# Laying out the first four chunks of a fused RWKV-5 and SwiGLU kernel anew: loading, tables, rounding and the order of the first blocks

## The chip, the cores and the metric

One core of one Trainium2 chip. The metric is device time in microseconds of one execution, lower is better. Times below are medians of several executions; a profile is one execution, and its span is about 1 to 2.5 us shorter than the time of the same execution.

Names: PE is TensorE (PEld its weight loads), DVE VectorE, ACT ScalarE, POOL GpSimd, SP SyncE.

## The reference

```python
# attention, B=4, H=8, S=768, D=48: y_t = r_t (state + u*k_t v_t^T); state = w*state + k_t v_t^T
x = attn_out.transpose(0, 2, 1, 3).reshape(B * S, H * D)          # 3072 x 384
rms = np.sqrt(np.mean(x * x, axis=-1, keepdims=True) + 1e-06)
xn = x / rms * rms_g
g = xn @ w_gate                                                   # 384 x 1536
out = (g / (1 + np.exp(-g)) * (xn @ w_val)) @ w_out               # 1536 x 384
```

The three large weights come as float64. The kernel loads them as 64-bit words and rounds them to float32 itself.

## The kernel before

The sequence is cut into 12 chunks of 64 tokens (times 4 batches). Chunks 0 and 1 are computed alone while the weights still arrive, later chunks in pairs ("pair blocks", 2 and 3 first). In the traces read here, PE, DVE and ACT instructions run in the program's order on each engine, so an instruction that stands early in the program holds up everything behind it on its engine.

The attention of a chunk is called by letters: `1 2 3` the bonus (TOK, TOK times u, reduced to du), `R K` the decayed r and k on DVE, `d` the diagonal (16 small ACT products a half), `a` the scores (tile pa), `m` the mask, `y` the outputs (py), `q r n` squares, root and norm (pm, rms, xa, xb), `h` the K-hat products (KH), `u` the state (pu). A capital means the second half.

```python
def decay_r(s):                                                    # "R"
    dve.tensor_mul(ME, CH[:, 0], ...up...)
    act.copy(MO[64:128], ME[64:128])
def decay_k(s):                                                    # "K"
    dve.tensor_mul(CH[:, 1], CH[:, 1], ...down...)
def diagonal(s, half):                                             # "d": eight products into ME, eight into MO
    ...
    act.mul(t[rows, b, p, :], dmask[rows], du[rows, x : x + 1])

def round_piece():                                                 # 24 pieces: 6 for each quarter of the weights
    dst, raw = staged.popleft()
    ...
    act.activation(ulp, lo, AF.Copy, scale=2.0**-29)
    dve.tensor_scalar(out=bits, in0=hi, scalar1=3, scalar2=0x3FFFFFF8, ...)
    dve.scalar_tensor_tensor(out=bits, in0=hi, scalar=-0x40000000, in1=bits, ...)
    nc.gpsimd.tensor_tensor(out=dst.bitcast(I32), in0=bits, in1=ulp, op=ALU.add)
    stage()                                                        # issues the load of the next piece

def gate_val(s, nn):                                               # needs pieces 0-3 of its quarter
    product(ps_, unit(wa[i], o), xa[s], True)
    product(ps_, unit(wb[i], o), xb[s], False)
    act.activation(h, ps_[:, 0, 0:NT], AF.Silu)
    dve.tensor_mul(h, ps_[:, 1, 0:NT], h)
# add_cell(q, s): h of three gate_val times a quarter of w_out; needs pieces 4 and 5 of its quarter

def check():                                                       # 48 of these, through ONE buffer: weights in range?
    raw = mine.tile([P, CHECK], I64, name=f"again_{n}", tag="again")
    nc.sync.dma_start(out=raw, in_=src[:, k * CHECK : (k + 1) * CHECK])
    act.activation(mag, hi, AF.Abs)
    act.activation(mag, mag, AF.Relu, ..., accum_out=seen[:, n : n + 1])
# at the end: bad = reduction of seen; every engine loads bad and branches (a general kernel for odd inputs)
```

The whole kernel:

## Time and profile before

| | |
|---|---|
| time | 748.5 us (median of 4, 747.7 to 749.4) |
| profiled span | 747.5 us |
| first b product of the pair blocks | 236.9 us |
| last projection product (po) ends | 740.0 us |
| TensorE before that first b, from 14 us on | 157.9 us busy, 65.0 us idle |
| TensorE at half clock before that first b | 75.6 us |

How to read it: the last three quarters of the kernel run TensorE nearly without a hole. The first b product: the first product of the pair blocks that needs sums of both chunks, so a good marker of where the beginning ends. "Idle" and "half clock" are taken from the trace: gaps between matmuls, and the records of the granted clock, which are 1.0 or 0.5.

### The profile page before, as it was taken

The page shows a single profiled execution, that of the slowest core. Times are in us where ns is not written, and L with a number is a line of the kernel's source. Part 1 is how long each engine was busy: PE and PEld are TensorE (multiplying, and loading weights), DVE is VectorE, ACT ScalarE, POOL GpSimd, SP SyncE. Part 2 cuts the span into 40 slices and gives each one's busy share as a digit, 9 for nine tenths or more (in the row PEclk, how much of TensorE's full clock was granted, in tenths as well). Part 3 has the DMA queues.
Part 4 walks back from the last instruction along what each step waited for, and adds up shares of the span by engine and source line. Part 5 has one row for each costly group of instructions (what it writes and reads, how often), then busy time and mean ns, then how long its engine had stood idle before and what let it go on. Part 6 is the DMA issues. An engine that isn't in the chain of part 4 may idle for free.

```text
span 747.5 us, 14896 instructions
## 1 busy us (share of the span) xinstructions
PE 654.6 (88%) x6326; PEld 502.6 (67%) x6326; DVE 400.3 (54%) x569; ACT 341.4 (46%) x945; POOL 45.1 (6%) x40
## 2 busy tenths in 40 slices
PE   2378468796697999999999999999999999999996
PEld 1255256564575778667888668887678886688853
DVE  5836355344537874736675646657257646445410
ACT  1443543534523352545565725746545647244400
POOL 4323112021100000000000000000000000000000
PEclk9768689897899999999999999999999999999999
DMA  8635245053042003242243413153431332022201
GB/s 220 169 108 164 63 107 174 7 132 108 12 116 59 1 1 86 49 101 70 63 130 83 89 55 96 51 148 78 98 73 51 111 87 65 22 59 65 64 21 26
DMA packets 20571, 61.31 MB, mean 82 GB/s; under 512 B 3984, under 2 KB 7056, under 8 KB 19344
## 3 DMA queue, kind: packets, MB, share of 16 engines
q1 hardware_dynamic: 20496, 60.28, 31.0%
q8 instruction: 51, 0.84, 0.5%
q14 instruction: 24, 0.20, 0.1%
HBM read 55.54 MB, written 4.72 MB: 81 GB/s over the span
## 4 chain that ended last, share of the span: by engine, by line
PE 77%; DVE 10%; ACT 5%; issue 4%; DMA 2%; POOL 1%; DVEq 0%; POOLq 0%; ACTq 0%
PE po L89 25%; PE b L89 14%; PE a L89 9%; PE gv L89 9%; PE c L89 8%; PE py L89 5%; PE pa L89 4%; PE pu L89 3%; DVE bits L89 2%; DVE gv L89 1%; ACT MO L89 1%; DMA chan<-in_chan_dram 1%; DVE rms L89 1%; DVE TOK L89 1%; DVE h L89 1%
## 5 line engine op out<-in xcount | busy, mean ns | idle before, releaser
L89 PE MATMUL po<-wo,h 128*128 128x384 f32 x576 | 199.4, 499 | 2.6 <-POOL wo L204 2.6
L89 PEld LDWEIGHTS po<-wo,h 128*128 128x128 f32 x576 | 108.6, 193 | 73.9 <-POOL wo L204 3.9
L89 DVE TENSOR_TENSOR gv<-b,m 128x512 f32<-128x512 f32 x90 | 62.1, 690 | 64.3 <-PE b L89 63.6
L89 PE MATMUL pa<-ME,chan 48*64 48x64 f32 x384 | 31.1, 240 | 32.3 <-issue 18.2
L89 PEld LDWEIGHTS pa<-ME,chan 48*64 48x64 f32 x384 | 27.9, 152 | 41.8 <-issue 39.6
L89 ACT ACTIVATE gv<-gv 128x512 f32<-128x512 f32 (+1 forms) x60 | 31.1, 519 | 48.7 <-DVE gv L89 48.7
L89 PE MATMUL gv<-xa,wa 64*128 64x256 f32 x288 | 47.6, 464 | 4.4 <-DVE xa L89 4.4
L89 DVE TENSOR_TENSOR h<-gv,h 128x256 f32<-128x256 f32 x24 | 10.2, 424 | 74.8 <-ACT h L89 74.7
L89 DVE TENSOR_TENSOR gv<-c,gv 128x512 f32<-128x512 f32 x60 | 41.4, 690 | 15.4 <-PE c L89 14.3
L89 ACT ACTIVATE ME<-dmask,du 64x64 f32<-64x64 f32 x176 | 43.8, 330 | 12.1 <-DVE du L89 11.6
L89 PE MATMUL a<-xa,wa 64*128 64x256 f32 x360 | 45.1, 383 | 4.7 <-DVE h L89 4.7
L89 PE MATMUL b<-t,s 64*128 64x256 f32 x360 | 45.4, 386 | 4.0 <-DVE t L89 3.7
L89 PE MATMUL b<-xa,wa 64*128 64x256 f32 x360 | 45.5, 385 | 0.6 <-DVE gv L89 0.6
L89 PE MATMUL b<-t,wb 64*128 64x256 f32 x360 | 44.5, 379 | 0.8 <-DVE gv L89 0.8
L89 ACT ACTIVATE MO<-dmask,du 64x64 f32<-64x64 f32 x176 | 44.4, 335 | 0.4
L89 PE MATMUL c<-xb,s 64*128 64x256 f32 x360 | 44.3, 378 | 0.0
L89 PEld LDWEIGHTS py<-ME,VS 128*64 128x64 f32 (+1 forms) x576 | 36.4, 136 | 11.3 <-issue 10.7
L89 PE MATMUL c<-t,s 64*128 64x256 f32 x360 | 43.9, 376 | 0.0
L89 PE MATMUL a<-xb,wb 64*128 64x256 f32 x360 | 43.9, 376 | 0.0
L89 PE MATMUL gv<-xb,wb 64*128 64x256 f32 x288 | 40.1, 407 | 3.1 <-POOL wb L204 3.1
L89 PE MATMUL py<-ME,VS 128*64 128x64 f32 (+1 forms) x576 | 39.9, 229 | 2.5 <-DVE MO L89 2.5
L89 PEld LDWEIGHTS gv<-xa,wa 64*128 64x128 f32 x288 | 32.7, 227 | 13.7 <-DVE xa L89 4.8
(101 smaller groups left out, 1049.5 us busy)
## 6 DMA issues: line engine op xcount, KB each, us to landing
TOK<-in_tok_dram SPq DMA_DIRECT2D x12, 768.0 KB, 4.5
chan<-in_chan_dram SPq DMA_DIRECT2D x24, 384.0 KB, 6.4
VS<-in_vpad_dram SPq DMA_DIRECT2D x24, 336.0 KB, 4.8
raw<-in_wka_dram SPq DMA_DIRECT2D x8, 576.0 KB, 4.3
raw<-in_wkb_dram SPq DMA_DIRECT2D x8, 576.0 KB, 3.9
raw<-in_wot_dram SPq DMA_DIRECT2D x8, 576.0 KB, 3.8
again<-in_wka_dram SPq DMA_DIRECT2D x16, 288.0 KB, 2.8
out_dram<-o SPq DMA_DIRECT2D x48, 96.0 KB, 2.2
```

Of the source, the lines that this page charges most:

```text
L89: return lambda *args, **kwargs: self.tc.keep_in_program_order(give(*args, **kwargs))
```

## The change

Its intent: have chunk 1's attention done while TensorE works on the first quarter of the weights, ahead of the second quarter; build tables and K-hat early; keep more float64 pieces in flight; keep TensorE's clock up with products of constants where it would idle. Two sets of checks move as well.

```diff
-    raws = loading.enter_context(tc.tile_pool(name="raws", bufs=3))
+    raws = loading.enter_context(tc.tile_pool(name="raws", bufs=6))
...
-            nc.sync.dma_start(out=wraw[...], in_=w_v[z])           # w, u, g: now from ACT's queue
+            act.dma_start(out=wraw[...], in_=w_v[z])
...
-    def token_tables():                                            # tables and K-hat constants: now at once
...
+    def warm(n):
+        t = ps_gv.tile([P, P], FP32, name=f"warm_{len(warmed)}", tag="c")
+        for _ in range(n):
+            pe.matmul(t, ones, ones, start=True, stop=True)
...
-    mix(0, "RK123aAdmyDMY")
-    rounding(2), mix(0, "qr"), rounding(2), mix(0, "n"), token_tables()
-    gate_val(0, 0), rounding(1), mix(0, "h")
-    gate_val(0, 1), rounding(1), mix(0, "Hu")
-    gate_val(0, 2), mix(0, "U"), rounding(2)
-    add_cell(0, 0), rounding(2)
-    gate_val(0, 3), mix(1, "12")
-    gate_val(0, 4), mix(1, "3Rd")
-    gate_val(0, 5), mix(1, "K"), rounding(1), mix(1, "aDm"), rounding(1)
-    add_cell(1, 0), mix(1, "AMyY"), ...
+    warm(20)
+    mix(0, "123RKaAdmyDM"), rounding(2), mix(0, "Yhq"), warm(4), mix(0, "rHuU")
+    rounding(2), mix(0, "n"), warm(16)
+    gate_val(0, 0), rounding(1), mix(1, "12")
+    gate_val(0, 1), mix(1, "3Rd")
+    gate_val(0, 2), mix(1, "K"), rounding(1), mix(1, "aD")
+    add_cell(0, 0), mix(1, "mAyMYhHqruU"), rounding(2), mix(1, "n"), warm(8)
+    gate_val(1, 0), rounding(1)
+    gate_val(1, 1), rounding(1)
+    gate_val(1, 2), rounding(1)
+    add_cell(0, 1), rounding(1)
+    gate_val(0, 3), mix(2, "1")
+    gate_val(0, 4), mix(2, "2")
+    gate_val(0, 5), mix(2, "3")
+    add_cell(1, 0), mix(2, "Rd")
+    gate_val(1, 3), mix(2, "K")
+    gate_val(1, 4), mix(2, "aDm"), rounding(1)
+    gate_val(1, 5), mix(2, "AM")
+    add_cell(1, 1), mix(2, "y"), rounding(1), mix(2, "Y"), rounding(2)
...                                                                 # chunk 3 in the same way
-                if not first_block and k in (2, 5):
+                if not first_block and k in (2, 5) and m != 2:
                     check()
...
-                project(s, j, False), project(s, j, True)
+                project(s, j, False), project(s, j, True), check(), check()
```

Not in this cut, but in the change: TOK's load goes out ahead of chan's, a Sqrt of a constant loads ACT's table early, and half of chunk 1's diagonal products (those into ME) move from ACT to DVE.

More of the change, by code (lines that the diff above doesn't have):

```diff
@@ L124, in fast @@
     dve.memset(wraw, 1.0)
+    eps = c_tile([P, 1], "eps")
+    dve.memset(eps, EPS)
     w_v = w.rearrange("(a e) d -> e d a", e=2)
@@ L127, in fast @@
         for z in range(2):
-            nc.sync.dma_start(out=wraw[64 * z : 64 * z + D, :], in_=w_v[z])
-    wcol = c_tile([P, HP], "wcol")
-    dve.tensor_scalar(out=wcol, in0=wraw, scalar1=W_LOW, scalar2=W_HIGH, op0=ALU.max, op1=ALU.min)
+            act.dma_start(out=wraw[64 * z : 64 * z + D, :], in_=w_v[z])
     CH = c_tile([P, 2, B, HP, L], "chan")
@@ L148, in load_v @@
         nc.sync.dma_start(out=VS[0:64, 1], in_=vpad[s, 0:64])
+    utab = c_tile([P, HP, D], "utab")
+    gcol = c_tile([P, CC], "gcol")
     for z in range(2):
-        nc.gpsimd.memset(CH[64 * z + 32 : 64 * z + 64], 0.0)
+        (dve, nc.gpsimd)[z].memset(CH[64 * z + 32 : 64 * z + 64], 0.0)
+    load_tok(0)
     load_chan(0)
-    load_tok(0)
-    utab = c_tile([P, HP, D], "utab")
     for z in range(2):
         src = bass.AP(tensor=u.tensor, offset=u.offset + z * D, ap=[[0, 64], [2 * D, HP], [1, D]])
-        nc.sync.dma_start(out=utab[64 - 64 * z : 128 - 64 * z], in_=src)
+        act.dma_start(out=utab[64 - 64 * z : 128 - 64 * z], in_=src)
+    act.dma_start(out=gcol, in_=g_cols)
+    spare = c_tile([P, 1], "spare")
+    act.activation(spare, eps, AF.Sqrt)
     wa = [c_tile([P, CC, NQ * P], f"wa_{i}") for i in range(WQ)]
@@ L212, in fast @@
     load_v(0)
-    stage()
-    stage()
-    stage()
-    gcol = c_tile([P, CC], "gcol")
-    nc.sync.dma_start(out=gcol, in_=g_cols)
+    for _ in range(6):
+        stage()
     ident = c_tile([P, P], "ident")
@@ L223, in fast @@
     nc.gpsimd.memset(ones, 1.0)
-    eps = c_tile([P, 1], "eps")
-    dve.memset(eps, EPS)
+    nc.gpsimd.memset(KH[32:64, 0], 0.0)
+    nc.gpsimd.memset(KH[96:128, 1], 0.0)
+    wcol = c_tile([P, HP], "wcol")
+    dve.tensor_scalar(out=wcol, in0=wraw, scalar1=W_LOW, scalar2=W_HIGH, op0=ALU.max, op1=ALU.min)
     dmask, mask = c_tile([P, L], "dmask"), c_tile([P, L], "mask")
@@ L238, in fast @@
     nc.gpsimd.memset(VS[64:128, 1], 0.0)
-    nc.gpsimd.memset(KH[32:64, 0], 0.0)
-    nc.gpsimd.memset(KH[96:128, 1], 0.0)
     pw = raws.tile([P, HP, L], FP32, name="pw", tag="pw", bufs=1)
@@ L262, in fast @@
     dve.tensor_add(dmask, ident[:, 0:64], ident[:, 64:128])
-    def token_tables():
-        for z in range(2):
-            dve.tensor_mul(gdup[:, :, z, :], pw_rev, free_dims(pows[L // 2], (1, HP), (0, L)))
-        ps = ps_at.tile([P, HP, P], FP32, name="ps_wk", tag="at")
-        for p in range(HP):
-            pe.transpose(ps[:, p, :], gdup[:, p].rearrange("c z t -> c (z t)"), ident)
-        act.copy(wk[64:128], ps[64:128, :, 0:D])
-        act.copy(wk[0:64], ps[0:64, :, 64 : 64 + D])
-        for z in range(2):
-            rows = slice(64 * z, 64 * z + D)
-            for p in range(HP):
-                act.mul(
-                    KH[rows, z, :, p, :], free_dims(ident[rows, 64 * z : 64 * z + D], (0, B), (1, D)),
-                    pows[L][rows, p : p + 1],
-                )
+    for z in range(2):
+        dve.tensor_mul(gdup[:, :, z, :], pw_rev, free_dims(pows[L // 2], (1, HP), (0, L)))
+    ps = ps_at.tile([P, HP, P], FP32, name="ps_wk", tag="at")
+    for p in range(HP):
+        pe.transpose(ps[:, p, :], gdup[:, p].rearrange("c z t -> c (z t)"), ident)
+    act.copy(wk[64:128], ps[64:128, :, 0:D])
+    act.copy(wk[0:64], ps[0:64, :, 64 : 64 + D])
+    for z in range(2):
+        rows = slice(64 * z, 64 * z + D)
+        for p in range(HP):
+            act.mul(
+                KH[rows, z, :, p, :], free_dims(ident[rows, 64 * z : 64 * z + D], (0, B), (1, D)),
+                pows[L][rows, p : p + 1],
+            )
     def w_range():
@@ L319, in diagonal @@
         for t, rows in ((ME, slice(64, 128)), (MO, slice(0, 64))):
-            if s == 0:
+            if s == 0 or (s == 1 and t is ME):
                 dve.tensor_mul(
@@ L517, in rounding @@
             round_piece()
-    mix(0, "RK123aAdmyDMY")
-    rounding(2)
-    mix(0, "qr")
-    rounding(2)
-    mix(0, "n")
-    token_tables()
-    gate_val(0, 0), rounding(1), mix(0, "h")
-    gate_val(0, 1), rounding(1), mix(0, "Hu")
-    gate_val(0, 2), mix(0, "U"), rounding(2)
-    count = w_range()
-    add_cell(0, 0), rounding(2)
-    gate_val(0, 3), mix(1, "12")
-    gate_val(0, 4), mix(1, "3Rd")
-    gate_val(0, 5), mix(1, "K"), rounding(1), mix(1, "aDm"), rounding(1)
-    add_cell(1, 0), mix(1, "AMyY"), rounding(1), mix(1, "qr"), rounding(1), mix(1, "n")
@@ L534, in fast @@
-    gate_val(1, 0), rounding(1), mix(1, "h")
-    gate_val(1, 1), mix(1, "Hu"), rounding(1)
-    gate_val(1, 2), mix(1, "U"), rounding(1)
-    add_cell(0, 1), mix(2, "12")
-    gate_val(1, 3), mix(2, "3Rd")
-    gate_val(1, 4), mix(2, "K")
-    gate_val(1, 5), mix(2, "aDm")
-    add_cell(1, 1), mix(2, "A"), rounding(1), mix(2, "M")
-    gate_val(0, 6), mix(2, "y"), rounding(1)
-    gate_val(0, 7), mix(2, "Y")
-    gate_val(0, 8), mix(2, "q"), rounding(1), mix(2, "r")
-    add_cell(2, 0), mix(2, "n")
@@ L546, in fast @@
-    gate_val(1, 6), mix(2, "hHu"), rounding(1)
-    gate_val(1, 7), mix(2, "U"), rounding(1)
-    gate_val(1, 8), mix(3, "12")
-    add_cell(2, 1), mix(3, "3Rd"), rounding(1)
-    gate_val(0, 9), mix(3, "K"), rounding(1)
-    gate_val(0, 10), mix(3, "aDm")
-    gate_val(0, 11), rounding(1), mix(3, "AM")
-    rounded(len(pieces))
+    def warm(n):
+        t = ps_gv.tile([P, P], FP32, name=f"warm_{len(warmed)}", tag="c")
+        warmed.append(t)
+        for _ in range(n):
+            pe.matmul(t, ones, ones, start=True, stop=True)
@@ new lines, in fast @@
+    warmed = []
+    warm(20)
[5 more added lines that the diff above has]
+    add_cell(0, 0), mix(1, "mAyMYhHqruU"), rounding(2), mix(1, "n"), warm(8)
+    count = w_range()
+    gate_val(1, 0), rounding(1)
+    gate_val(1, 1), rounding(1)
+    gate_val(1, 2), rounding(1)
+    add_cell(0, 1), rounding(1)
@@ new lines, in fast @@
+    gate_val(0, 3), mix(2, "1")
[6 more added lines that the diff above has]
+    add_cell(1, 1), mix(2, "y"), rounding(1), mix(2, "Y"), rounding(2)
+    gate_val(0, 6), mix(2, "qr")
+    gate_val(0, 7), mix(2, "n")
+    gate_val(0, 8), rounding(2), mix(2, "h")
+    add_cell(2, 0), mix(2, "Hu"), rounding(1)
+    gate_val(1, 6), mix(2, "U"), mix(3, "1")
@@ L554, in fast @@
+    gate_val(1, 7), mix(3, "2"), rounding(1)
+    gate_val(1, 8), mix(3, "3Rd")
+    add_cell(2, 1), mix(3, "K"), rounding(1), mix(3, "aD"), rounding(1)
+    gate_val(0, 9), mix(3, "mA")
+    gate_val(0, 10), mix(3, "My"), rounding(1)
+    gate_val(0, 11), mix(3, "Y"), rounding(1)
+    assert state["done"] == len(pieces)
     loading.close()
@@ L666, in project @@
             store(osb, s + j // 2, j % 2)
-    add_cell(3, 0), mix(3, "h")
-    gate_val(1, 9), mix(3, "yH")
-    gate_val(1, 10), mix(3, "Y"), sum_1(0)
-    gate_val(1, 11), mix(3, "q"), sum_2(0), mix(3, "r")
-    add_cell(3, 1), mix(3, "nuU")
-    token_sum(2, 1), token_sum(2, 2)
+    add_cell(3, 0), mix(3, "qr"), sum_1(0)
+    gate_val(1, 9), mix(3, "n")
+    gate_val(1, 10), mix(3, "h"), sum_2(0)
+    gate_val(1, 11), mix(3, "Hu"), token_sum(2, 1)
+    add_cell(3, 1), mix(3, "U"), token_sum(2, 2)
     for s in range(FIRST, NS, 2):
```

## The prediction

> **What bounds the kernel now.** I read the busy slices and the granted clock first, then the same split by stages, then the waits of TensorE, then ScalarE's timeline in front of the longest of them, then the timeline of the end.
>
> The page's second part (40 slices of 18.7 us):
>
> ```profile
> PE   2378468796697999999999999999999999999996
> PEclk9768689897899999999999999999999999999999
> ```
>
> From about slice 13 (237 us) on, TensorE is full at full clock. Before that it has holes, and the clock sags with them. Busy time by stage (start:end, length, busy us and instructions of PE, PEld, DVE, ACT, POOL, then clock, DMA share, GB/s):
>
> ```profile
> 27.00:79.00 52.00, 31.13 (x226) 22.76 (x226) 27.74 (x35) 22.00 (x47) 15.51 (x10) 0.74 0.45 143
> 79.00:106.00 27.00, 13.67 (x175) 9.27 (x175) 13.62 (x20) 13.60 (x43) 6.07 (x4) 0.70 0.43 108
> 106.00:175.00 69.00, 54.02 (x504) 40.81 (x504) 31.19 (x43) 29.76 (x74) 9.13 (x6) 0.87 0.32 89
> 175.00:237.00 62.00, 50.09 (x530) 38.10 (x530) 30.34 (x41) 23.95 (x71) 5.61 (x4) 0.89 0.34 86
> 237.00:700.00 463.00, 456.58 (x4556) 357.15 (x4558) 272.95 (x380) 239.90 (x688) 0.00 (x0) 1.00 0.28 72
> ```
>
> No engine is full before 237 us, so latencies in series bound that part: TensorE is busy about 158 of 237 us, some of it at half rate. Priced at warm rates (a gate_val 2.79 us x24, an add_cell 4.07 x8, some 30 us of attention products) its work there is only about 130 us. The other 107 us are what the change can shorten. The waits of TensorE in 0 to 200 us (us in total, times, longest):
>
> ```profile
> PE pa L89 <- DVE chan L89: 14.1, 1, 14.1
> PE pu L89 <- DVE KH L89: 13.2, 6, 6.0
> PE pa L89 <- issue: 12.2, 2, 7.4
> PE ps_wk L89 <- ACT xb L89: 10.5, 1, 10.5
> ```
>
> The waits "pa <- issue" are not free time: ScalarE's timeline shows what runs in the longest, 76.1 to 83.5 us. The copy into MO and 16 small products stand ahead of the Silu whose h then holds up VectorE's K product:
>
> ```profile
> 76.44 1.04 ACT L89 COPY MO<-ME 64x1024 f32<-64x1024 f32 x1 [2.48 <-DVE ME L89]
> 77.51 1.99 ACT L89 ACTIVATE ME<-dmask,du 64x64 f32<-64x64 f32 x8
> 79.52 2.02 ACT L89 ACTIVATE MO<-dmask,du 64x64 f32<-64x64 f32 x8
> 81.44 0.36 ACT L89 ACTIVATE h<-gv 128x256 f32<-128x256 f32 x1
> ```
>
> The end: VectorE has written the flag "bad" at 740.3, long before the last output has landed.
>
> ```profile
> 740.06 0.48 ACT L89 COPY o<-po 128x384 f32<-128x384 f32 x1 [7.26 <-PE po L89]
> 740.13 0.14 DVE L729 CAST bad<-pc 1x1 int32<-1x1 f32 x1 [28.09 <-PE pc L728]
> 740.56 1.11 SPq L475 DMA_DIRECT2D out_dram<-o  x2
> ```
>
> **What the Trainium skill says.** (1) "TensorE: Matmul & The Clock Gate", What's actually happening: the array runs at half clock after an idle window of about 3.4 us and at full clock after about as long busy. The trace agrees: clock records are 0.5 or 1.0 in multiples of 3.41 us. Full clock returned 3 to 6 us after work resumed (resumed 50.5, full at 55.5; resumed 175.4, full at 181.8), and the 1.8 us holes at 159 and 224 us left it full. A resumption costs about 2 us. (2) "SBUF — State Buffer", SBUF: two separate sides: VectorE and GpSimd share a port pair as a lock. The trace agrees: the second step of a piece's rounding takes 0.76 us, but 1.84 beside a GpSimd add. (3) "ScalarE: Activation LUTs", What ACT_TABLE_LOAD costs: about 1283 ns; the trace has 1.28. (4) "Runtime: NRT & Kernel Launch", Instruction fetch mechanics: a taken branch outside the fetched window stalls. TensorE's closing branch takes 4.53 us in the trace, from 740.91.
>
> **The change part by part.** I walk through the new order by hand, each instruction taking its duration in the old trace.
>
> *Start.* w is issued first, from ScalarE's queue, so the tables begin near 6.5 instead of 7.16 us. But the gdup products (0.7) and the token chain (2.9) now stand on VectorE before R and K (2.3), and ScalarE's wk copies and eight KH products (0.6+3.0) before the MO copy. The transposes start at 11.1; MO is there at 16.9. A 128-column product is about a third of the po one (0.68 us warm), 0.23 warm and 0.45 cold, so the 20 warming products last from 12.2 to 18.3-19.2. The scores follow warm, and the last mask of chunk 0 ends near 24 us, against 22.8: **1 us lost**.
>
> *Chunk 0 to its third gate_val.* KH is already there, so pu runs right after pm, the 16 warming products end at 37.5, and gate_val(0,0) starts there warm instead of cold at 39.1. The state products no longer interrupt. gate_val(0,2) and pu are over at 45.9 against 57.3: **11 us won**.
>
> *Chunk 1 brought forward.* R, MO copy, half the diagonal and the Silu run in series again: K is ready at 52.7, so TensorE idles 6.8 us and restarts cold (about 2). add_cell(0,0) ends near 60, the outputs at 64, pu at 67.6, and gate_val(1,0) starts at 71.4 after xa, xb and 8 warming products. In the old kernel it starts at 106.0. To compare I add to the new one the work it hasn't done (three gate_val and an add_cell, 12.5), and to the old one its later pu and that one's waits (4): 110 against 84, so **26 us won so far**. This is the main gain: the half-empty second stage (13.7 busy of 27 us) goes, since rounding of the second quarter and chunk 1 no longer alternate.
>
> *Chunk 2.* TensorE now runs gate_val and add_cell unbroken from 71 to 102. The MO/diagonal wait recurs (3.5 us, old 4.8), then pieces 13 to 15 are rounded late (about 3), and add_cell(2,0) waits for pieces 16 and 17 (about 6). pu of chunk 2 starts at 148.5 with one gate_val (2.8) still owed, against 175.4: the lead is **24 us**.
>
> *Chunk 3.* ScalarE rounds piece 21 only after 16 diagonal products (4.4 us of wait), piece 23 only after the last outputs (3.4), and KH comes late (4.2), while the old kernel's waits of 6.0, 1.8 and 3.7 go. The first b product of the pair blocks falls at about 215.7 against 236.9: **21 us won**.
>
> *Pair blocks.* Three of them stall 1.1 us each after group 2, where a check (1.1 us on ScalarE) joins the 4 us of diagonal products. Leaving the check out there wins about **3 us**.
>
> *End.* Eight checks move beside the last projection, through one buffer. With T the end of TensorE's work: output copy to T+0.55, check 46 to T+1.0, the load of check 47 behind the two stores at T+1.7, landed at T+4.5 (2.8 us, section 6 of the page), its two passes to T+5.7, reductions, pc and cast to T+6.7. The flag was at T+0.3. All engines branch on it, so the end moves by about 6.4 us: **6 us lost**.
>
> Sum: 747.7 - 21 - 3 + 6 = about 730 us.
>
> **The rivals.** *A: the waits only move.* The rounding pieces are as many as before (24, each about 1.2 us VectorE, 0.7 ScalarE, 1.4 GpSimd), and chunk 3 now collects them. For it: VectorE and ScalarE are ordered queues, and the wait before pa occurs three times in the old trace. Then the lead falls to 10-12 us: about 740. *B: the clock pays more than I count.* In 27 to 106 us the clock is 0.70 to 0.74; with the warming products it could hold through 37 to 100 us, and if late rounding hides behind products, the lead is 28-30: about 722. Against it: the 6.8 us hole before pa of chunk 1 has no warming product. *C: the loads bind.* Six raw pieces of 0.59 MB now go out with 2.3 MB of chunk data; at the 183 GB/s of the first 27 us that is 32 us of transfer. Pieces 2 and 3 are wanted at about 30, so a delay of 2-4 us is possible: about 733. *D: the flag is earlier than I think*, or its branch hides behind the last store: 726.
>
> **Range and chances.** The hand walk has some forty steps with an error of perhaps 5 us at its end; the tail adds 2, the pair blocks 1. Between A and B I expect 730, with 719 to 742 as range. The line for 2% is 732.8, only 3 us above, hence faster 0.64, same 0.34. Slower by over 2% would need the lead gone and more: 0.02.
>
> **What would show it.** Right if gate_val(1,0) starts at 68-75 us, the first b product of the pair blocks at 210-221, the stalls before group 3 shrink in three blocks, and the flag is cast over 5 us after the last po product. Wrong if piece adds on GpSimd release most waits of TensorE in 100-200 us for longer than the 17 us I give them (A), if the clock stays 1.0 from 18 to 100 us (B), if rounding waits on DMA (C), or if the flag is cast within 2 us of the last product (D).

## More of the kernel before

All kernels named here gave correct results.

## The result, and the profile after

739.7 us (median of 4, 737.3 to 740.3) against 748.5: 8.8 us less, where 18 were predicted. The ratio is 0.9876 (95% interval 0.9849 to 0.9903). A ratio here is the mean time of one kernel's runs over that of the other's of the same rounds, so it is not quite the ratio of the medians. The forecast range (719 to 742) holds the time, at its slow edge; the more likely class, faster by over 2%, did not come. All outputs are right.

The busy slices and the granted clock of the changed kernel (40 slices of 18.4 us):

```profile
PE   4668978586879899999999999999999999999992
PEclk9888998787899999999999999999999999999997
```

Slices 4 and 5 (55 to 92 us) are now at 8 and 9 tenths (8 and 4 before); slices 6 to 12 are as ragged as before. The stages (start:end, length, busy us and instructions of PE, PEld, DVE, ACT, POOL, then clock, DMA share, GB/s), cut at the first gate_val of chunk 1, before chunk 2's scores, at the first pu of chunk 2, at the first b product and at the last po product:

```profile
27.00:73.06 46.06, 33.61 (x425) 27.59 (x425) 30.90 (x40) 22.58 (x57) 9.64 (x6) 0.81 0.53 148
73.06:106.00 32.94, 30.49 (x216) 22.92 (x216) 16.64 (x23) 13.85 (x32) 9.00 (x6) 1.00 0.40 121
106.00:153.92 47.92, 33.36 (x282) 22.77 (x283) 21.73 (x30) 17.04 (x42) 9.17 (x6) 0.79 0.34 91
153.92:225.96 72.04, 55.91 (x555) 41.73 (x556) 33.97 (x47) 27.60 (x77) 8.42 (x6) 0.88 0.21 54
225.96:724.20 498.24, 494.48 (x4734) 381.98 (x4730) 278.75 (x390) 243.29 (x693) 0.00 (x0) 1.00 0.27 70
```

The second line is the change's success: 33 us with TensorE 93% busy at full clock. In the same stretch DVE and ACT are only half busy (16.6 and 13.9 us). The third line is where it is lost: 33 of 48 us busy, at 0.79 of the clock. The waits of TensorE from 100 us to the first b product (us in total, times, longest):

```profile
PE po L89 <- POOL wo L209: 10.2, 3, 6.4
PE pu L89 <- DVE KH L89: 6.0, 3, 2.2
PE gv L89 <- POOL wb L209: 5.5, 3, 3.4
PE pa L89 <- DVE chan L89: 3.8, 1, 3.8
PE pm L89 <- DVE sq L89: 3.8, 2, 1.9
PE pa L89 <- issue: 2.2, 1, 2.2
PE gv L89 <- POOL wa L209: 1.1, 1, 1.1
```

The three lines with POOL, 16.8 us together, are rounded pieces that come too late. In 0 to 200 us of the kernel before, POOL ended 5.7 us of waits. One of them on ACT, and then on POOL:

```profile
173.84 0.71 ACT L89 ACTIVATE ulp<-raw 128x576 int32<-128x576 uint32 x1
174.58 1.99 ACT L89 ACTIVATE ME<-dmask,du 64x64 f32<-64x64 f32 x8
176.58 2.02 ACT L89 ACTIVATE MO<-dmask,du 64x64 f32<-64x64 f32 x8
178.51 0.70 ACT L89 ACTIVATE ulp<-raw 128x576 int32<-128x576 uint32 x1
```
```profile
179.28 1.40 POOL L209 TENSOR_TENSOR wb<-bits,ulp 128x576 int32<-128x576 int32 x1 [3.25 <-ACT ulp L89]
```

Piece 21's ulp stands behind 16 diagonal products in the program, so its add ends at 180.7, and gate_val, which needs it, waits from 177.3 to 180.7.

The end (times from the start of the span; the last po product ends at 724.2):

```profile
724.24 0.48 ACT L89 COPY o<-po 128x384 f32<-128x384 f32 x1 [1.83 <-PE po L89]
...
725.95 0.55 SPq L583 DMA_DIRECT2D again<-in_wot_dram  x1
729.00 0.46 ACT L89 ACTIVATE mag<-again 128x288 f32<-128x288 f32 x1 [3.23 <-DMA again<-in_wot_dram]
...
730.95 0.14 DVE L733 CAST bad<-pc 1x1 int32<-1x1 f32 x1 [0.28 <-PE pc L732]
```

The last check's load is issued only behind the two stores and behind the check ahead of it (one buffer); the flag is ready 6.9 us after the last product, where it was 0.3.

The sum of the profiled spans: the first b product comes 10.96 us earlier (236.92 to 225.96), the pair blocks take 4.82 less (503.06 to 498.24), the end takes 6.15 more (7.50 to 13.65). Together -9.6, from 747.5 to 737.9.

### The profile page after: what moved, and what is told of

Its sections match the earlier page's. It is cut to its first block, busy times and chain, and to the rows that moved or that the text cites. A ratio compares the mean times of both kernels' runs of the same rounds, so it can differ in the third digit from the quotient of the medians.

```text
span 737.9 us, 15078 instructions
## 1 busy us (share of the span) xinstructions
PE 662.3 (90%) x6422; PEld 510.7 (69%) x6422; DVE 402.4 (55%) x572; ACT 336.8 (46%) x929; POOL 44.7 (6%) x39
## 4 chain that ended last, share of the span: by engine, by line
PE 77%; DVE 11%; ACT 6%; issue 3%; POOL 1%; DMA 1%; SPq 0%; ACTq 0%; DVEq 0%; POOLq 0%
PE po L89 26%; PE b L89 14%; PE a L89 9%; PE c L89 9%; PE gv L89 7%; PE py L89 4%; PE pa L89 4%; PE pu L89 2%; ACT MO L89 2%; ACT ME L89 2%; PE warm L89 2%; DVE bits L89 2%; DVE h L89 1%; DVE gv L89 1%; DVE ME L89 1%
## 5 line engine op out<-in xcount | busy, mean ns | idle before, releaser
L89 PE MATMUL po<-wo,h 128*128 128x384 f32 x576 | 203.1, 505 | 10.2 <-POOL wo L209 10.2
L89 ACT ACTIVATE ME<-dmask,du 64x64 f32<-64x64 f32 x160 | 39.8, 330 | 12.0 <-DVE du L89 11.6
L89 PE MATMUL gv<-xa,wa 64*128 64x256 f32 x288 | 42.5, 428 | 1.9 <-POOL wa L209 1.1
L89 PEld LDWEIGHTS pa<-ME,chan 48*64 48x64 f32 x384 | 26.6, 146 | 23.3 <-issue 16.8
L89 PE MATMUL gv<-xb,wb 64*128 64x256 f32 x288 | 37.4, 391 | 5.7 <-POOL wb L209 5.5
L89 PEld LDWEIGHTS py<-ME,VS 128*64 128x64 f32 (+1 forms) x576 | 34.4, 130 | 10.9 <-issue 10.5
L89 ACT COPY VS<-pu 48x288 f32<-48x288 f32 x88 | 23.2, 312 | 39.1 <-PE pu L89 38.7
L89 PE MATMUL py<-ME,VS 128*64 128x64 f32 (+1 forms) x576 | 37.7, 222 | 2.3 <-DVE MO L89 2.3
```

The costliest lines, as they stand in the source:

```text
L89: return lambda *args, **kwargs: self.tc.keep_in_program_order(give(*args, **kwargs))
```

## The experiments

Theory A: what is missing of the forecast gain sits in chunks 2 and 3, where late rounding holds TensorE, and the placing of the checks gives away 6 us at the end. Rival E: ACT's and DVE's ordered queues are the bound there, so a wait taken away comes back under another name. Rival D: the late flag costs nothing.

An overview first; "first b" and "end" (from the last po product to the end) are from each run's trace. The start of the first products varies between executions by up to 1.6 us with the landing of w (10.0 to 11.6 us), so differences in "first b" of under 2 us are not read.

| run | time, us | ratio to before | first b, us | end, us |
|---|---|---|---|---|
| before | 748.5 | 1 | 236.9 | 7.5 |
| the change | 739.7 | 0.9876 | 226.0 | 13.7 |
| tail_early | 733.8 | 0.9802 | 226.0 | 7.6 |
| round_early | 724.1 | 0.9647 | 209.8 | 13.4 |
| both | 717.1 | 0.9579 | 212.1 | 7.6 |
| no_warm | 741.4 | 0.9904 | 229.1 | 13.1 |
| old_order | 742.3 | 0.9913 | 227.8 | 13.9 |
| bufs3 | 739.0 | 0.9860 | 225.7 | 13.9 |
| warm8 | 740.1 | 0.9886 | 226.6 | 13.5 |
| checks_only | 752.1 | 1.0050 | 235.6 | 13.4 |
| warm_fill | 711.8 | 0.9510 | 204.8 | 7.3 |
| k_first | 705.0 | 0.9424 | 197.0 | 7.6 |
| kh_early | 693.3 | 0.9256 | 185.7 | 7.6 |

### The end: tail_early and checks_only

tail_early, on the changed kernel:

```diff
-                if not first_block and k in (2, 5) and m != 2:
+                if not first_block and k in (2, 5) and (m != 2 or n == NS):
...
-                project(s, j, False), project(s, j, True), check(), check()
+                project(s, j, False)
+                if j < 3:
+                    check()
+                project(s, j, True)
+                if j < 3:
+                    check()
```

> The changed kernel, with the eight late checks moved so that none lies behind the last projection: two in group 2 of the last pair block, six beside the first three projections. Theory (the flag's late check holds up the end): the flag is ready when the last product ends, the end after it shrinks from 13.7 to about 7.5 us, 739.7 falls by 6 us to 733.5 or so. Rival (the branch hides behind the last store, or the drain is long anyway): within 1.5 us of 739.7. Either way TensorE's time up to its last product stays within 1 us.

Measured 733.8, 5.9 less than the change. The last check now ends well ahead of the last product (ends at 724.24):

```profile
717.76 0.19 ACT L89 ACTIVATION_READ_ACCUMULATOR mag<-mag 128x1 f32 x1
717.98 0.19 DVE L728 TENSOR_SCALAR tiny<-seen 128x48 f32<-128x48 f32 x1 [23.09 <-ACT mag L89]
```

The first b product and the 498.24 us of the pair blocks are unchanged; only the end shrank, from 13.65 to 7.58 us. Rival D falls.

checks_only puts the changed placing of the checks, and nothing else, into the kernel before (the two last hunks of the diff above).

> The kernel before with the changed placing of the checks alone. Theory (6.2 us more behind the last product, three stalls of 1.1 us fewer): 3 to 4 us longer than before, about 752. Rival (the flag's branch hides behind the last store in this kernel): 2.8 us shorter, about 745.

Measured 752.1, 3.4 longer than the kernel before in the same rounds (748.6; ratio 1.0050, interval 1.0031 to 1.0069). Its flag:

```profile
742.42 0.15 DVE L729 CAST bad<-pc 1x1 int32<-1x1 f32 x1 [0.28 <-PE pc L728]
```

That is 7.0 us after its last po product (735.58). The pair blocks took 499.95 us instead of 503.06, so leaving the checks out of group 2 is worth 3.1 us, and the end costs 5.9 more. As placed, this part of the change is a loss.

### The middle: round_early, both

round_early rounds pieces 12 to 15 in the stretch where DVE and ACT are half idle, and the later ones earlier in turn:

```diff
-    gate_val(0, 3), mix(2, "1")
-    gate_val(0, 4), mix(2, "2")
-    gate_val(0, 5), mix(2, "3")
+    gate_val(0, 3), mix(2, "1"), rounding(1)
+    gate_val(0, 4), mix(2, "2"), rounding(1)
+    gate_val(0, 5), mix(2, "3"), rounding(1)
...
-    add_cell(1, 1), mix(2, "y"), rounding(1), mix(2, "Y"), rounding(2)
+    add_cell(1, 1), mix(2, "y"), rounding(1), mix(2, "Y"), rounding(1)
...
-    gate_val(0, 8), rounding(2), mix(2, "h")
+    gate_val(0, 8), rounding(1), mix(2, "h")
...
-    gate_val(1, 8), mix(3, "3Rd")
-    add_cell(2, 1), mix(3, "K"), rounding(1), mix(3, "aD"), rounding(1)
-    gate_val(0, 9), mix(3, "mA")
+    gate_val(1, 8), rounding(1), mix(3, "3Rd")
+    add_cell(2, 1), mix(3, "K"), mix(3, "aD")
+    gate_val(0, 9), mix(3, "mA"), rounding(1)
...
-    gate_val(0, 11), mix(3, "Y"), rounding(1)
+    gate_val(0, 11), mix(3, "Y")
```

> The changed kernel, with pieces 12 to 15 rounded during 86 to 106 us, where VectorE and ScalarE are half idle, and the later ones moved up in their place. Theory A (late rounding is what holds TensorE in 106 to 226 us, 16.8 us of waits on GpSimd's adds plus cold restarts): those waits fall below 5 us and the first b product of the pair blocks moves from 226 to 213-217, time about 729. Rival E (ScalarE's diagonal products and VectorE's queue would hold it anyway, so the waits only change their name): waits on POOL fall but those of pa, pu and pm grow, the first b product stays at 222 or later, time 736 or more.

Measured 724.1 (three executions 723.4 to 725.0, one of 715.9; the interval is 0.9583 to 0.9710), and the first b product moved by 16 us, more than expected. Waits of TensorE from 100 us to the first b product, the largest:

```profile
PE pu L89 <- DVE KH L89: 6.0, 3, 2.2
PE pm L89 <- DVE sq L89: 3.8, 2, 1.9
PE pa L89 <- DVE chan L89: 3.8, 1, 3.8
PE pa L89 <- issue: 3.7, 1, 3.7
PE po L89 <- DVE h L89: 2.1, 1, 2.1
```

No wait on POOL is left of the 16.8 us, and the others grew by only 3.6 (2.1 for h, 1.5 before pa). TensorE's idle time from 106 us to the first b product fell from 30.7 to 17.2 us. Late rounding did hold TensorE there, as theory A has it, and rival E explains at most those 3.6 us. But the forecast had counted the waits for pieces too, at 16.8 us, so they are not what it missed (see the part on the prediction). The time lost to the half clock hardly fell: half of TensorE's busy time in half-clock stretches is 15.4 us in the change and 14.1 here.

> Both edits together. Theory: they act in different stages and add up, about 723 us (739.7 - 6 - 10). Under rival E about 732.

Measured 717.1, against 739.7 - 5.9 - 15.7 = 718.1: the two edits add up, as they act in different stages.

### The parts of the change: old_order, bufs3, no_warm, warm8

old_order keeps the new start, the six buffers and the new checks, and puts the old sequence back from gate_val(0,0) to the end of chunk 3 (the lines with a minus in the diff of the change, without the parts that are done earlier now).

> The changed kernel with the old order of chunk 1 and of everything after it (from gate_val(0,0) on), the new start kept: tables first, six buffers, products of constants before chunk 0, checks as changed. Theory: the new order won some 12 to 15 us by the first gate_val of chunk 1 and lost them again by rounding late, so the first b product falls at 224 to 230, as in the changed kernel (226), time 737 to 744. Rival (the new order is worth its full 15 us even so, the start nothing): first b at 235 or later, time 750.

Measured 742.3, and the first b product at 227.8. Midway the new order was far ahead: chunk 1's first gate_val comes at 73.1 instead of 96.4 us, with three gate_val and an add_cell (12.5 us) still owed, less 4 us for pu of chunk 1 and its waits, which the old order still has ahead. That is a lead of 96.4 + 4 - 73.1 - 12.5 = 14.8 us. At the first b product 1.9 us of it are left, less than is read here (old_order's first product starts at 11.6 us, the change's at 10.0). The new order as delivered is worth 2.5 us of time; about 9.1 us of the first b's 11.0 come with the new start (236.9 to 227.8), which here includes the six buffers and chunk 1's diagonal products on DVE.

bufs3 is the changed kernel with `bufs=3` for the pool and `for _ in range(3): stage()`.

> The changed kernel with three buffers for float64 pieces and three pieces staged, as before. Theory (pieces are rounded 3 to 10 us apart in the new order, a load takes 4 to 6 us, so three in flight suffice): 0 to 2 us longer, 739.7 to 742. Rival (six buffers are what lets chunk 1's loads pass the second quarter's): 5 us or more longer.

Measured 739.0, with the first b product at 225.7: the six buffers are worth nothing here.

no_warm lets `warm` return at once; warm8 lets it return unless n is 8.

> The changed kernel without its 48 products of constants. Theory (they keep the clock up for the first gate_val and the attention products after them): at half clock the outputs of chunk 0, pu and the first gate_val take about 3 to 5 us more, but the scores of chunk 0 start 1 us earlier; time 2 to 4 us longer, 742 to 744. Rival (the waits behind them absorb the difference, since xa and the rounded pieces set the start of gate_val anyway): within 1 us of 739.7.

> The changed kernel with only the last eight of its 48 products of constants, those before chunk 1's gate_val. Theory (the first 40 delay what follows as much as the clock they keep is worth, gate_val(1,0) came at 73.4 us without any against 73.1 with all; the last eight keep the clock up for 12 us of gate_val): the time of all 48 within 1 us, 738.7 to 740.7. Rival (the gain of 1.6 us is spread over all of them): 741 or more.

Without any products of constants 741.4, with the last eight alone 740.1, with all 739.7. So all 48 are worth about 1.6 us (the intervals of the two ratios, 0.9849 to 0.9903 and 0.9887 to 0.9920, overlap), and the 40 in front 0.4 at most, which is within the spread. gate_val(0,0) starts at 35.6 us in no_warm and at 38.8 in the change: the sixteen products keep the clock but stand in the way of the work they are to speed up. no_warm's forecast of 742 to 744 was a little too dark.

### The next waits: warm_fill and k_first

Both stand on `both`, and both treat the same three holes before the scores of chunks 1, 2 and 3 (7.2, 3.8 and 3.7 us). warm_fill leaves the holes and keeps the clock up in them (in the third, 2.5 us pass before its products start); k_first takes their cause away.

```diff
 warm_fill
-    gate_val(0, 2), mix(1, "K"), rounding(1), mix(1, "aD")
+    gate_val(0, 2), mix(1, "K"), rounding(1), warm(30), mix(1, "aD")
...
-    gate_val(1, 4), mix(2, "aDm"), rounding(1)
+    gate_val(1, 4), warm(15), mix(2, "aDm"), rounding(1)
...
-    add_cell(2, 1), mix(3, "K"), mix(3, "aD")
+    add_cell(2, 1), mix(3, "K"), warm(11), mix(3, "aD")
```

> Both earlier edits, and the same three holes filled with products of constants (30, 15 and 11) instead. Theory (a hole[...] costs its length and then about 2 to 3 us more at half clock): the holes keep their end, but what follows runs at full clock, 717 falls by 5 to 8 us to 709-712. Rival (what follows the hole waits for pieces and ScalarE anyway): under 2 us gained.

Measured 711.8, 5.2 less than `both`. TensorE ran at half clock for 23.9 us up to the first b product, where `both` did for 47.8. A hole's second cost, the restart at half clock, is real and can be had back alone.

```diff
 k_first
-    gate_val(0, 1), mix(1, "3Rd")
-    gate_val(0, 2), mix(1, "K"), rounding(1), mix(1, "aD")
+    gate_val(0, 1), mix(1, "3RK"), rounding(1), mix(1, "d")
+    gate_val(0, 2), mix(1, "aD")
...
-    add_cell(1, 0), mix(2, "Rd")
-    gate_val(1, 3), mix(2, "K")
+    add_cell(1, 0), mix(2, "RKd")
+    gate_val(1, 3)
...
-    gate_val(1, 8), rounding(1), mix(3, "3Rd")
-    add_cell(2, 1), mix(3, "K"), mix(3, "aD")
+    gate_val(1, 8), rounding(1), mix(3, "3RKd")
+    add_cell(2, 1), mix(3, "aD")
```

> Both earlier edits, and K's product on VectorE right behind R, ahead of the diagonal products, in chunks 1 to 3; piece 5 ahead of the diagonal too. Theory (the scores wait for K, K for the h ahead of it on VectorE, that h for the Silu behind 16 diagonal products on ScalarE): the holes before the scores of 7.2, 3.8 and 3.7 us shrink to 3.5, under 1 and under 1 us, the cold restarts behind them go too, 717 falls to 705-710. Rival (ScalarE's queue as a whole is the bound, so the next thing behind the diagonal waits as long): 714 or more.

Measured 705.0, 12.1 less than `both`, at the good end of what was expected. Waits of TensorE from 46 us to the first b product, the largest:

```profile
PE pa L89 <- issue: 6.2, 2, 3.4
PE pu L89 <- DVE KH L89: 6.0, 3, 2.2
PE pm L89 <- DVE sq L89: 5.4, 3, 1.9
```

Before the scores of chunk 2 no wait is left; 3.4 us remain at chunk 1 and 2.8 at chunk 3. The scores had not waited for ACT's products themselves but for K, which stood behind an h on DVE, and that h behind a Silu behind those products. In chunk 1 piece 5 was moved as well, and the two moves have no runs apart. For chunk 3 the forecast (under 1 us) missed: 2.8 us stayed. The table calls that wait "issue", but the timeline shows K ending 0.1 us before it does:

```profile
151.54 1.21 DVE L89 TENSOR_TENSOR chan<-chan,down 128x1024 f32<-128x1024 f32 x1
152.85 0.30 PE L89 MATMUL pa<-ME,chan 48*64 48x64 f32 x2 [2.78 <-issue]
```

On DVE, K stands there behind an h, a piece's rounding, du and R, without a gap from 146.5 us on.

### A version that beats both kernels: kh_early

On k_first: the K-hat products of chunks 2 and 3 are moved ahead of adds and norms on DVE, norm 2 goes behind add_cell(2,0), and 14 products of constants fill the hole before chunk 1's scores.

```diff
-    gate_val(0, 2), mix(1, "aD")
+    gate_val(0, 2), warm(14), mix(1, "aD")
...
-    gate_val(0, 7), mix(2, "n")
-    gate_val(0, 8), rounding(1), mix(2, "h")
-    add_cell(2, 0), mix(2, "Hu"), rounding(1)
+    gate_val(0, 7), mix(2, "hH")
+    gate_val(0, 8), rounding(1)
+    add_cell(2, 0), mix(2, "u"), rounding(1), mix(2, "n")
...
-    gate_val(0, 11), mix(3, "Y")
+    gate_val(0, 11), mix(3, "YhH")
...
-    gate_val(1, 10), mix(3, "h"), sum_2(0)
-    gate_val(1, 11), mix(3, "Hu"), token_sum(2, 1)
-    add_cell(3, 1), mix(3, "U"), token_sum(2, 2)
+    gate_val(1, 10), mix(3, "u"), sum_2(0)
+    gate_val(1, 11), mix(3, "U"), token_sum(2, 1), token_sum(2, 2)
+    add_cell(3, 1)
```

> The version of 705.0 us, with the K-hat products of chunks 2 and 3 moved ahead of the adds and norms that stood before them on VectorE, norm 2 moved behind add_cell(2,0), and 14 products of constants in the hole before chunk 1's scores. Theory (pu waited 6.0 us for those products, po 2.1 us for an h behind norm 2, with two cold restarts): 705 falls by 6 to 10 us to 695-699. Rival (the norm or the o add takes the place): 702 or more.

Measured 693.3 (691.9 to 693.9), 11.7 less than k_first and a little more than expected; ratio to the kernel before 0.9256. What each of the three moves is worth has no run. The busy slices (17.3 us each) and the clock:

```profile
PE   3697988988998999999999999999999999999995
PEclk9899999999999999999999999999999999999999
```

TensorE was at half clock for 13.7 us up to the first b product, against 54.6 in the change and 75.6 before.

## Why the prediction was right or wrong

- **What bounds the kernel.** Right. The beginning is a chain of latencies: edits that move a few instructions on DVE, ACT and POOL and add no work for them took 46 us out of it (739.7 to 693.3, 6 of them at the end).
- **The start.** Right within 1 to 2 us. The tables began earlier than taken (5.9 us), the transposes at 10.0 for 11.1; the last mask of chunk 0 ended at 23.5 for "near 24". gate_val(0,0) started at 38.8 for 37.5. That the start does win was confirmed by old_order (9.1 us).
- **Chunk 1 brought forward.** Right: gate_val(1,0) at 73.1 for 71.4, the hole before its scores 7.2 for 6.8 us, and the lead there about 24 us for 26.
- **Chunks 2 and 3.** Here the sum was mis-sized, and this is the miss. "The lead is 24 us" measured 18.7 at pu of chunk 2 (175.4 - 153.9 - 2.8), and "21 us won" measured 10.96 at the first b product. The waits that the text names were right: 24.5 us, measured 24.8 (pieces 16.7 for 16.8, the scores of chunk 2 3.8 for 3.5, KH of chunk 3 4.3 for 4.2). What failed is that four more waits of TensorE were left out, 7.7 us together: pm of both chunks for the squares (1.8 and 1.9), pu of chunk 2 for KH (1.7) and the scores of chunk 3 (2.2). For chunk 3 the text says that the old kernel's waits of 6.0 and 1.8 us "go"; 2.2 and 1.9 us stayed. The half clock is not the miss, in sum: between its 71.4 and 215.7 us the text leaves 144.3 - 24.5 = 119.8 us beside the named waits, and TensorE was busy for 119.8 us from 73.06 to 225.96, with 37.5 us at half clock (which cost 15.4) among them. Of the 10.3 us by which the first b product came late, 1.7 were there at gate_val(1,0) and about 1 lies in smaller gaps.
- **Pair blocks.** Right: the three stalls of 1.1 us shrank to 0.19 each. checks_only prices this at 3.1 us for "about 3". The change's pair blocks gained 4.8; most of the other 1.7 us (1.4 by old_order) goes with a first b product that no longer waits and starts at full clock (old_order, where it waits 3.7 us as in the kernel before, has 499.6 us for the change's 498.2).
- **The end.** Right: the flag at 6.9 us after the last product for 6.7, the end 6.15 us later for 6.4.
- **Rivals.** A (the waits move to the rounding) came nearest in its number, about 740, but by luck: waits of TensorE on POOL from 100 us to the first b product were 16.8 us, about the 17 that the text itself put in, so its own test did not trip, and what was missing lay in other waits. B fell: the clock did hold from 60 to 108 us, but sank afterwards, and late rounding did not hide. C fell: from 0 to 230 us of the change no engine's wait on a piece's load shows (ACT and DVE of the kernel before have 3.0 us), and three buffers do as well as six. D fell with tail_early.
- **What the text did not see:** the order of chunks 1 to 3 could be had with 16 us more by moving rounding calls alone, and the six buffers and 40 of the 48 products were worth nothing. It took the change's parts for one thing, and never priced buffers and products by themselves.

## What to carry to other kernels

When work is brought forward, ask what used to stand in the stretch that it now fills and where that has gone: here the rounding of the later weights slid behind the work that needed it, and a 15 us lead shrank to about 2, although DVE and ACT stood half idle just before. On engines that keep their order, look behind the instruction that a wait names to the one that stood in front of it (K behind an h, the h behind a Silu, the Silu behind sixteen small products) and move the one that others wait for, not the one that is slow. When an order is walked by hand, take the old trace's waits one by one and say of each why it goes: the four not walked here were 7.7 of the 10.3 us missed. And keep anything that a final branch depends on clear of the last stage: a check of 1 us of work cost 6 us there, through one buffer and a load.

## What the Trainium skill lacked or had wrong

- "TensorE: Matmul & The Clock Gate", What's actually happening, names an idle window of about 3.4 us as what halves the clock, and does not say how much work a window may hold and still count as idle. The runs show it halved after shorter holes: in round_early TensorE was idle from 125.3 to 127.2 us (1.9 us) and the clock was half from 127.4 to 130.8; the window of 3.4 us that ended there held 1.5 us of work. In k_first a hole of 1.9 us (118.1 to 120.0), whose window (116.4 to 119.9) held 1.6 us of work, left the clock full. Cut into such windows along the edges of the clock records, up to 260 us, the thirteen traces show no window with more than 1.84 us of work after which full clock became half, and none with less than 1.50 us after which it stayed full; in between both happen.
- "Runtime: NRT & Kernel Launch", Instruction fetch mechanics, says that a taken branch out of the fetched window stalls, without a figure. From the closing branch to an engine's next instruction the traces show 2.7 to 4.6 us (before) and 3.4 to 4.0 us (the change), on every engine. That the fetch is what takes this time no run here shows.
